# Moving a complex chunk scan from GpSimd to VectorE beside a ScalarE-paced attention

## The chip, the cores and the metric

The kernel runs on one NeuronCore of a Trainium2 chip. The metric is the device time of one execution in microseconds (us); smaller is better. Every run is repeated, and the kernel before runs beside it on the same chip. Engines are named as in the profile: PE is TensorE, PEld its weight loads, DVE VectorE, ACT ScalarE, POOL GpSimd, SPq the queue of DMA issues on SyncE.

## The reference

The output mixes two branches of the same input `x` (2048 positions, 512 channels, bf16):

```python
g = sigmoid((x * gate_w).sum(-1, keepdims=True))
a = softmax_attention(x, wqkv, heads=32, Dh=16) @ wo       # no mask, 2048 x 2048 scores per head
b = causal_conv(x, K) + x * Dskip                          # an S4 state-space convolution
#   K[d, l] = Re( sum_n C[d,n] * exp(dt[d] * A[d,n] * l) * dt[d] * B[d,n] ),  n = 0..127
return g * a + (1 - g) * b
```

Attention needs 32 x 2048 x 2048 exponentials. The convolution is done in 32 chunks of 64 positions. With `lam = exp(dt*A)`, a state of 128 complex numbers per channel is carried from chunk to chunk: `G <- mu * G + S[c]`, where `mu = lam^64` and `S[c]` is the contribution of chunk c. Inside a chunk the 64 taps of `K` are used directly.

## The kernel before

A small scheduler in the kernel writes the order of every engine. There are 512 steps. Each has a fixed attention part: two 128x1024 exponentials on ScalarE, the score matmuls of the next step, the value matmuls of the step before. What the convolution needs is squeezed in between by threads that ask for TensorE, VectorE or GpSimd time (`yield ("DVE", .7)`), for an event (`AFTER`), for a step (`Q`) or for the one free PSUM bank `MB` (`LOCK`). The engines then run their lists in order, each waiting on semaphores. Step numbers in this text are the scheduler's; times are the trace's.

```python
for q in range(NQ):                      # NQ = 512
    ex(2 * q)                            # ScalarE, 128x1024
    if q + 1 < NQ: qk(q + 1)             # TensorE: scores into PSUM banks SC
    ex(2 * q + 1)
    rate = dict(PE=.62 if q > 50 else 1.0, DVE=1.5, POOL=1.8)
    ...                                  # pv(q-1): values into PSUM bank OA; every 16 steps norm()
    sch.step(rate)                       # the convolution's threads
```

The threads that matter, in order of time:

```python
def base(qr, eng, k, c1):    # powers lam^0..15 of one quarter (128 channels), f32; quarter 0 on DVE, 1 to 3 on POOL
    ...
def table():                 # per block of 32 channels (16 blocks): lam^0..63 into PT, bf16, on DVE
    for blk in range(NBLK):
        ...
        for m in range(1, 4):
            for part in range(2):
                yield ("DVE", 1.05)      # three 128x512 bf16 tensor_tensor
                ...
def kstage(blk):             # taps K = Re(W * lam^l): 32 matmuls of 128 columns into MB, evicted to Kst, 8 DMAs
    ...
def sstage(blk):             # chunk sums S: 4 banks of MB per block, each evicted to Sst and sent to memory
    for bank in range(4):
        yield ("LOCK", "MB")
        yield ("PE", .6)
        ...                                          # 4 matmuls Ut x Qt into MB
        yield ("DVE", .7)
        op("DVE", ... v.tensor_copy(Sst(512 * (bank % 2), [[1, 512]]), MB(0, [[1, 512]])) ...)
        sch.unlock("MB")
        dma("SP", ... sd.dram(...), Sst(512 * (bank % 2), ...))
def weigh():                 # DVE: SW = W * S for four chunks at a time, 6 f32 operations
    ...
def scan():                  # POOL: per chunk s2 = G*Re(mu); s3 = swap(G)*Im(mu); s2 += SW; G = s2 + s3; SG = bf16(G)
    ...
def ystage():                # per block: 16 pairs k; for each 1 matmul Uy x Tt and 4 matmuls SG x Py into MB
    ...                      # two column groups of the array at a time
def ublocks():               # reversed copies of x, built by GpSimd
    for qr in range(4):
        ...                                          # 2 DMAs into X2
        yield ("Q", 2 + 8 * qr)
        for par in range(2):
            yield ("POOL", 3.0)
            op("POOL", ... g.tensor_copy(UB(...), X2(...)))
def gate():
    yield ("Q", 8)
    for lt in range(16):
        dma("SP", ... xg <- 128 rows of x)           # two buffers
        yield ("DVE", .7)
        op("DVE", ... gp[lt] = sum(xg * gw))
    op("ACT", ... ge = Exp(-gp))                     # one small exponential in ScalarE's list
    ...
    yield ("AFTER", "scan2", 0)
    for lt in range(16):
        dma("SP", ... xh <- 128 rows of x)           # two buffers
        yield ("POOL", 1.2)
        op("POOL", ... xD[lt] = xh * Dskip)
```

`SG`, the scanned states, has two buffers for four quarters: the states of quarter 2 may be loaded only when the output taps of quarter 0 (blocks y0 to y3) are done, those of quarter 3 after y4 to y7.

The softmax here doesn't subtract the row's maximum and nothing guards it: scores larger than these inputs give would overflow.

## Time and profile before

The kernel takes 1259.88 us (median of 3 runs, 1259.55 to 1261.51).

| | before |
|---|---|
| profiled span, mean TensorE clock | 1261.5 us, 0.565 |
| busy: TensorE, VectorE, ScalarE, GpSimd | 818.9, 664.4, 967.4, 622.4 us |
| ScalarE idle just before attention's exponentials | 263.9 us, of it 230.7 until scores came |
| one step where nothing disturbs | about 1.835 us, so 512 steps take about 940 us |
| before the first exponential, after the last | 17.8 us, 13.3 us |

No engine is busy all the time, yet one sets the pace. The page of the kernel before, first the busy times, then four of its costliest groups (line, engine, operation, count; busy us, mean ns of one; idle time of that engine just before them and what ended it):

```profile
span 1261.5 us, 16332 instructions
...
PE 818.9 (65%) x6378; PEld 247.3 (20%) x6400; DVE 664.4 (53%) x958; ACT 967.4 (77%) x1032; POOL 622.4 (49%) x704
...
L519 ACT ACTIVATE ET<-SC 128x1024 bf16<-128x1024 f32 x1024 | 960.9, 1067 | 263.9 <-PE SC L426 230.7
...
L842 POOL TENSOR_TENSOR s_143<-G,MI 128x256 f32<-128x256 f32 x120 | 104.1, 868 | 0.0
...
L812 DVE SCALAR_TENSOR_TENSOR SW<-SW,sw_145 128x512 f32<-128x512 f32 (+1 forms) x64 | 51.5, 843 | 0.0
```

The first group is the pace: 1024 exponentials, 961 us, and 264 us in which ScalarE stood before one of them. Nearly all those waits were for scores, that is for TensorE. The waits say why TensorE was late (who waited for whom: us in total, times, longest):

```profile
ACT ET L519 <- PE SC L426: 230.7, 81, 17.0
...
PEld MB L426 <- DVE Sst L757: 105.1, 62, 10.8
...
DVE Sst L757 <- DMA gm_sd<-Sst: 20.8, 7, 6.5
```

TensorE works in order, so a convolution matmul that waits for the bank `MB` to be emptied by VectorE also holds up the scores behind it. And VectorE was late partly because of GpSimd. The same bf16 128x512 product of the table, grouped by shape, in the kernel before: first on blocks whose tables were made while GpSimd scanned, then on blocks while it was idle:

```profile
L544 DVE TENSOR_TENSOR tt_134<-B_130,D_116 128x512 bf16<-128x512 bf16 x8 | 7.2, 902 | 0.0
...
L544 DVE TENSOR_TENSOR tt_134<-B_128,D_116 128x512 bf16<-128x512 bf16 x8 | 3.4, 419 | 0.0
```

The page "SBUF — State Buffer" of the Trainium skill, section "Who interferes with whom", says that a VectorE instruction with two SBUF inputs contends with a GpSimd instruction that reads SBUF, and that one with at most one SBUF input, outside VectorE's 2-port modes, does not. This trace agrees: the two-input product takes 902 ns instead of 419, while the evictions from PSUM (`Sst`) take 0.69 us with GpSimd busy or idle.

### The profile page before, as it was taken

To read this page: it belongs to the slowest core of one execution; us is meant where nothing else is said; L and a number is where in the kernel's file an instruction comes from. 1 tells how busy PE (TensorE), PEld (TensorE's weight loads), DVE (VectorE), ACT (ScalarE), POOL (GpSimd) and SP (SyncE) were. 2 spreads that over 40 slices of the span, in tenths; PEclk is the share of its full clock that TensorE was granted. 3 is DMA by queue.
4 is the path that set the end of the run, shared out by engine and by line. 5 is a ranking of instruction groups with operands and counts; after the bars stand their busy time and mean duration, and the time that the engine had idled before them with its cause. 6 is when DMAs were issued, how large, how long until landed. Compare 5 with 4: busy or idle time off the path is not lost.

```text
span 1261.5 us, 16332 instructions
## 1 busy us (share of the span) xinstructions
PE 818.9 (65%) x6378; PEld 247.3 (20%) x6400; DVE 664.4 (53%) x958; ACT 967.4 (77%) x1032; POOL 622.4 (49%) x704
## 2 busy tenths in 40 slices
PE   5554665666766545456457898576489559967665
PEld 1111111111111111011112343231034114311111
DVE  5999883664566778977862010544454511041101
ACT  5545666987988667677669988479679778999995
POOL 3799770000009888889830000899999984000000
PEclk9867656755555555555555555555555555557855
DMA  9551001266753443122343546336024205100000
GB/s 218 107 128 44 1 8 51 69 196 166 155 151 72 111 102 92 46 81 63 88 121 92 161 112 136 81 105 140 0 59 118 63 17 150 27 5 26 22 1 17
DMA packets 227550, 107.30 MB, mean 85 GB/s; under 512 B 190097, under 2 KB 217233, under 8 KB 223377
## 3 DMA queue, kind: packets, MB, share of 16 engines
q1 hardware_dynamic: 225744, 104.55, 33.1%
q10 hardware_dynamic: 1728, 1.70, 0.5%
q8 instruction: 50, 0.82, 0.3%
q14 instruction: 28, 0.22, 0.1%
HBM read 42.34 MB, written 35.85 MB: 62 GB/s over the span
## 4 chain that ended last, share of the span: by engine, by line
DVE 36%; POOL 18%; PE 18%; ACT 17%; DMA 5%; issue 3%; SPq 2%; ACTq 0%; DVEq 0%; POOLq 0%
ACT ET L519 17%; PE MB L426 8%; PE SC L426 5%; DVE SW L800 4%; PE OA L426 4%; DVE sw_145 L805 4%; POOL s_142 L839 4%; POOL G L848 4%; POOL s_142 L845 4%; DVE tt_133 L544 4%; DVE tt_134 L544 4%; DVE PT L544 3%; POOL s_143 L842 3%; DMA gm_sd<-Sst 2%; DVE pt_115 L544 2%
## 5 line engine op out<-in xcount | busy, mean ns | idle before, releaser
L519 ACT ACTIVATE ET<-SC 128x1024 bf16<-128x1024 f32 x1024 | 960.9, 1067 | 263.9 <-PE SC L426 230.7
L426 PE MATMUL SC<-Qm,KT 32*128 32x512 bf16 x2048 | 300.0, 576 | 181.1 <-ACT ET L519 165.8
L426 PE MATMUL OA<-ET,VE 128*32 128x512 bf16 x2048 | 296.6, 583 | 23.4 <-DVE OT L534 22.2
L426 PEld LDWEIGHTS SC<-Qm,KT 32*128 32x128 bf16 x2048 | 55.2, 98 | 372.3 <-ACT ET L519 323.6
L842 POOL TENSOR_TENSOR s_143<-G,MI 128x256 f32<-128x256 f32 x120 | 104.1, 868 | 0.0
L845 POOL TENSOR_TENSOR s_142<-s_142,SW 128x256 f32<-128x256 f32 x120 | 103.5, 862 | 0.0
L848 POOL TENSOR_TENSOR G<-s_142,s_143 128x256 f32<-128x256 f32 x120 | 97.2, 810 | 9.3
L839 POOL TENSOR_TENSOR s_142<-G,MU 128x256 f32<-128x256 f32 x120 | 101.5, 845 | 0.0
L426 PE MATMUL MB<-Qt,Ut 128*64 128x256 bf16 x256 | 40.8, 420 | 91.6 <-DVE Sst L757 72.2
L534 DVE STREAM_TRANSPOSE OT<-OA 128x512 f32<-128x512 f32 x32 | 22.8, 713 | 142.5 <-PE OA L426 142.5
L426 PEld LDWEIGHTS OA<-ET,VE 128*32 128x32 bf16 x2048 | 54.1, 101 | 221.1 <-issue 193.0
L426 PE MATMUL MB<-Tt,Uy 128*64 128x64 bf16 x256 | 66.9, 261 | 31.3 <-DVE Yst L905 30.6
L773 POOL MEMSET SG_139<- 128x256 bf16 x2 | 0.6, 311 | 174.9 <-PE MB L426 174.9
L757 DVE CAST Sst<-MB 128x512 bf16<-128x512 f32 x64 | 44.1, 689 | 63.9 <-PE MB L426 43.1
L905 DVE CAST Yst<-MB 128x512 bf16<-128x512 f32 x16 | 11.0, 689 | 111.2 <-PE MB L426 111.2
L800 DVE TENSOR_TENSOR SW<-SG_140,WR 128x512 f32<-128x512 bf16 (+1 forms) x32 | 33.2, 1076 | 65.2 <-POOL SG_140 L851 54.7
L836 POOL COPY G<-SW 128x256 f32<-128x256 f32 x4 | 4.8, 1200 | 121.0 <-DVE SW L812 120.7
L800 DVE TENSOR_TENSOR SW<-SG_139,WR 128x512 f32<-128x512 bf16 (+1 forms) x32 | 29.6, 965 | 64.3 <-POOL SG_139 L851 45.0
L544 DVE TENSOR_TENSOR PT<-tt_133,tt_134 128x512 bf16<-128x512 bf16 x96 | 53.2, 554 | 3.3
L426 PE MATMUL MB<-Py,SG_140 128*32 128x64 bf16 x512 | 46.4, 271 | 8.6 <-POOL SG_140 L851 8.6
L426 PE MATMUL MB<-xT,Wk 128*128 128x512 bf16 x59 | 23.9, 495 | 42.7 <-DVE KT L492 15.6
L812 DVE SCALAR_TENSOR_TENSOR SW<-SW,sw_145 128x512 f32<-128x512 f32 (+1 forms) x64 | 51.5, 843 | 0.0
(192 smaller groups left out, 985.7 us busy)
## 6 DMA issues: line engine op xcount, KB each, us to landing
gm_ptd<-PT SPq DMA_DIRECT2D x16, 1024.0 KB
Py<-gm_ptd SPq DMA_DIRECT2D x16, 1024.0 KB
gm_sd<-Sst SPq DMA_DIRECT2D x64, 128.0 KB
X_146<-gm_xrd SPq DMA_DIRECT2D x8, 512.0 KB
gm_ud<-UB SPq DMA_DIRECT2D x4, 1024.0 KB
Ut<-gm_ud SPq DMA_DIRECT2D x16, 256.0 KB
Uy<-gm_ud SPq DMA_DIRECT2D x16, 256.0 KB
Tt<-gm_kpd SPq DMA_DIRECT2D x32, 128.0 KB
```

What stands on the lines that cost most here:

```text
L426: op("PE", lambda t: t.matmul(out(), lhsT(), rhs(), start=start, stop=stop, skip_group_check=True, **kw), R, W)
L519: op("ACT", lambda a: a.activation(ET(1024 * e, [[1, 1024]]), sc(0, [[1, 1024]]), AF.Exp, scale=DH ** -0.5), [(sc, 0, h // 2), (sc, 1, h / ...
L534: op("DVE", lambda v: v.transpose(OT(o, [[1, 512]]), OA(0, [[1, 512]])), [(OA, 0, b)], [(OT, 0, b)])
L544: op(eng, lambda v: v.tensor_tensor(o(), a(), b_(), f), R, W)
L757: op("DVE", lambda v, bank=bank: v.tensor_copy(Sst(512 * (bank % 2), [[1, 512]]), MB(0, [[1, 512]])), [(MB, 0, ('S', blk, bank))], [(Sst, ...
L800: op("DVE", lambda v, so=so, o=o, nc_=nc_, ri=ri: v.tensor_tensor(SW(o + 128 * ri, [[256, nc_], [1, 128]]), sg(so + 128 * ri, [[256, nc_], ...
L805: op("DVE", lambda v, so=so, nc_=nc_, ri=ri: v.tensor_tensor(sw2(128 * ri, [[256, nc_], [1, 128]]), sg(so + 128 * (1 - ri), [[256, nc_], [ ...
L812: op("DVE", lambda v, d=d, x=x, ri=ri: v.scalar_tensor_tensor(d(), d(), -1.0 if ri else 1.0, x(), ALU.mult, ALU.subtract), [(SW, (sl, ri), ...
L839: op(e, lambda v: v.tensor_tensor(s2(0, [[128, 2], [1, 128]]), G(0, [[128, 2], [1, 128]]), MU(d0, [[0, 2], [1, 128]]), ALU.mult), key("G", ...
L842: op(e, lambda v: v.tensor_tensor(s3(0, [[128, 2], [1, 128]]), G(128, [[-128, 2], [1, 128]]), MI(d0, [[D, 2], [1, 128]]), ALU.mult), key(" ...
L845: op(e, lambda v, o=o: v.tensor_tensor(s2(0, [[1, 256]]), s2(0, [[1, 256]]), SW(o, [[1, 256]]), ALU.add), [(s2, 0)] + swk, [(s2, 0)])
L848: op(e, lambda v: v.tensor_tensor(G(0, [[1, 256]]), s2(0, [[1, 256]]), s3(0, [[1, 256]]), ALU.add), [(s2, 0), (s3, 0)], [(G, 0)])
```

## The change

The intent: take the scan and the powers away from GpSimd, so that VectorE is no longer slowed; pay for VectorE's extra work by deleting the weighing pass; and shorten TensorE's small matmuls. The weight is removed by folding its complex square root `V` into the power table: if every entry is `V * lam^j`, then a chunk sum times an output tap carries `V * V = W` by itself. That needs a complex square root (two ScalarE `Sqrt`, one VectorE reciprocal) and a sign change of the imaginary half, which is done while `Sst` is evicted. The diff cut to its core:

```diff
-def base(qr, eng, k, c1):
+def base(qr, eng, c1):
...
-        op(eng, lambda v: v.memset(FP(0, ...), 1.0), ...)          # lam^0, lam^1
-        op(eng, lambda v: v.tensor_copy(FP(1, ...), B["L1"](d0, ...)), ...)
+        for l, n in ((0, "VV"), (1, "VL")):                         # V, V*lam
+            op(eng, lambda v, l=l, n=n: v.tensor_copy(FP(l, ...), B[n](d0, ...)), ...)
...
     def params():
+        ...
+        op("ACT", lambda a: a.activation(B["u3"](0, [[1, D]]), B["u1"](0, [[1, D]]), AF.Sqrt), ...)
+        ...
+        yield ("Q", p.q + 2)
+        yield ("DVE", .7)
+        tt("DVE", full("u1"), full("u2"), full("u3"), ALU.add, ...)
+        op("ACT", lambda a: a.activation(B["u3"](0, [[1, D]]), B["u1"](0, [[1, D]]), AF.Sqrt, scale=.5), ...)
+        ...
+        op("DVE", lambda v: v.reciprocal(B["u1"](0, [[1, D]]), B["u3"](0, [[1, D]])), ...)
...
     def table():
-                    yield ("DVE", 1.05)
+                    yield ("DVE", 1.27)
...
     def kstage(blk):             # 8 matmuls of 512 columns instead of 32 of 128, 1 DMA instead of 8
-        for k0 in range(0, 16, 4):
+        for part, wn in ((0, "wrb"), (1, "nwi")):
+            for a in range(4):
+                mm(lambda a=a: MB(0, [[1, 512]], 32 * a, 32), ...)
...
     def sstage(blk):
-            op("DVE", ... v.tensor_copy(Sst(512 * (bank % 2), [[1, 512]]), MB(0, [[1, 512]])) ...)
+            op("DVE", ... v.tensor_copy(Sst(..., [[256, 2], [1, 128]]), MB(0, [[256, 2], [1, 128]])) ...)
+            op("DVE", ... v.tensor_scalar(Sst(... + 128, [[256, 2], [1, 128]]), MB(128, ...), -1.0, None, ALU.mult) ...)
...
-    def weigh():                                                    # deleted, 40 lines
     def scan():
-                e = "POOL"
+        e = "DVE"
+            for bl in range(4):
+                yield ("AFTER", f"sg{4 * qr + bl}", 4)
...
     def ystage():                # half blocks; per q: 2 matmuls Uy x Tt, then 8 of SG x Py over four column groups
-                for par in range(2):
-                    for ri in range(2):
+                for ri in range(2):
+                    for j in range(4):
...
     def gate():
-        yield ("AFTER", "scan2", 0)
+        yield ("AFTER", "S15", 0)
...
-    for th in (projs(), params(), base(0, "DVE", 0, .00105), table(), weigh(), scan(), ystage(), ...):
+    for th in (projs(), params(), scan(), bases(), table(), ystage(), ublocks(), gate(), combine(), outs()):
...
-        rate = dict(PE=.62 if q > 50 else 1.0, DVE=1.5, POOL=1.8)
+        rate = dict(PE=.62 if q > 50 else 1.0, DVE=1.65, POOL=1.8)
```

The tables now wait for the powers of all four quarters (`base3`), not only of their own.

## The prediction

> **What bounds the kernel now.** ScalarE paces it: 512 steps of two 128x1024 exponentials. Where nothing disturbs them (timeline, last 80 us) a pair takes 1.84 us, so 512 take about 940 us, plus 18 us of head and 13 us of tail: a floor near 970 us. The page's groups show 264 us of ScalarE idle before these exponentials, 231 of them ended by TensorE's scores. TensorE (819 us busy, clock 0.565) runs in order and stalls at the bank MB until VectorE empties it (waits: 105 us for Sst, 31 Yst, 35 KT). VectorE is late mostly because of GpSimd. From windows and timeline, per 16 steps (floor 29.4 us): steps 0-63, powers on both engines, 44 to 56 us; steps 64-143, tables and chunk sums, 29 to 37; steps 144-239, GpSimd scan with VectorE weighing, 39 to 49; taps (y) 33 to 36; one reload of SG at 768-791 us, 50.
>
> **GpSimd's cost to VectorE.** A bf16 128x512 tensor_tensor takes 0.42 us alone, 0.84 overlapped by GpSimd; f32 128x1024 1.22 against 2.6; the weighing products 0.68 against 1.2. The Trainium skill ("SBUF — State Buffer", Who interferes with whom) says that a VectorE instruction with two SBUF inputs contends with a GpSimd instruction that reads SBUF; this trace agrees.
>
> **Removed.** 409 us of GpSimd scan, about 110 us of GpSimd powers, VectorE's 132 us of weighing, the doubling by overlap, and on TensorE 384 narrow matmuls (40 us busy become about 18).
> **Added.** The scan on VectorE: estimated from its 128x256/512 operations 0.33 to 0.43 us each, about 1.75 us per chunk, 124 chunks, 215 us. Three more quarters of powers, about 25 us each; a square root of the weight, about 15 us; two ScalarE square roots, with up to four table loads of 1.28 us. Sst's eviction becomes two operations, 0.69 to 0.85 us.
>
> **What lies on the path.** By the program's order and uncontended durations, VectorE needs 22 to 31 us per 16 steps nearly everywhere (38 in the first 16): about ScalarE's 29.4. So:
> - steps 0-15: about 48; 16-95: 31 to 36 (before 29 to 56);
> - tables and chunk sums: 31 to 32; scans 32 to 33, since VectorE about equals ScalarE;
> - taps: 10 small matmuls cost 0.97 us in pairs now; four column groups at once should need about 0.5, so a step (0.54+0.54+0.5) drops under 1.84: 31 to 32;
> - given back: scans 2 and 3 each start 4 steps after the taps that free their SG buffer, while the reload needs about 20 us; each loses some 8 to 12 us (before only once); scans 0 and 1 a few us;
> - tail: five output tiles in one bank now stand after the last exponential: about +13 us.
> Sum: about 1105 us, 12% less.
>
> Predicted 1105 us, 8 in 10 between 1055 and 1165. Faster by over 2%: 0.94; within 2%: 0.04; slower: 0.02.
>
> **What would show it.** GpSimd busy under 110 us; bf16 table products at 0.42 us throughout; ScalarE idle near 130 us; scan windows at 31-34 us per 16 steps, taps at 30-33; two idle ScalarE stretches at starts of scans 2 and 3; 24-28 us after the last exponential.
>
> **What would make it wrong.** VectorE's scan slower than 1.75 us per chunk, stalling each softmax normalization; the SP queue filled by twice as many tap loads (about 13 of 15 us per block); chunk-sum stages staying at 2.2 us per step through the Sst handoff.

## The result, and the profile after

The changed kernel takes 1168.95 us (median of 4 runs, 1164.44 to 1170.63), and its result is correct. The ratio to the kernel before is 0.927 (95% interval 0.924 to 0.930). Ratios here are the mean time of one kernel's fast runs over that of the other's of the same rounds, so not quite the ratio of the medians quoted. The gain is 91 us, where the prediction had 155. The direction was right; the time lies just outside the range of 1055 to 1165.

The page after, the same groups:

```profile
span 1168.8 us, 15477 instructions
...
PE 755.2 (65%) x5997; PEld 204.7 (18%) x6016; DVE 671.8 (57%) x1525; ACT 978.9 (84%) x1039; POOL 64.4 (6%) x36
...
L515 ACT ACTIVATE ET<-SC 128x1024 bf16<-128x1024 f32 x1024 | 965.5, 1104 | 120.0 <-PE SC L422 107.9
...
L829 DVE TENSOR_TENSOR G<-s_138,s_139 128x256 f32<-128x256 f32 x120 | 51.0, 425 | 4.1
```

VectorE does the whole scan and is hardly busier than before (672 us against 664), because the weighing and the doubled durations are gone. ScalarE's idle time before attention's exponentials fell from 264 to 120 us. The mean clock granted to TensorE was 0.591, against 0.565 before; no run tells what that is worth, but the scan windows below show no higher clock after (0.50) than before (0.53). The waits:

```profile
ACT ET L515 <- PE SC L422: 107.9, 49, 8.5
PEld MB L422 <- DVE Sst L780: 81.4, 61, 5.6
...
DVE Sst L778 <- DMA gm_sd<-Sst: 30.5, 12, 4.3
...
DVE G L819 <- DMA SG_136<-gm_sd: 19.5, 2, 17.8
...
ACT ge L945 <- DVE gp L941: 17.6, 1, 17.6
DVE G L819 <- DMA SG_135<-gm_sd: 17.2, 1, 17.2
```

Two of these stand out: a VectorE wait of 17 to 18 us for reloaded states at each of two scans, which was predicted (before there was one such wait, of 19.3 us), and a single ScalarE wait of 17.6 us for the gate (5.5 us before), which was not. The table product of the kernel after, by shape, no longer depends on the block:

```profile
L540 DVE TENSOR_TENSOR tt_131<-B_128,D_119 128x512 bf16<-128x512 bf16 x8 | 3.4, 419 | 0.0
```

Where the time went is best seen by steps. The starts of the exponentials cut the trace into stretches; the predicted column is worked out from the prediction's figures per 16 steps (the middle of a range where it gave one; for "taps, scans 2 and 3" nine windows of 31.5 and three of 32.5, plus 20 for the two reloads). The columns of the trace add up to the spans within 0.2 us; the predicted one adds up to about 1100, not quite the 1105 of the prediction's own sum.

| steps (stage in the kernel after) | before, us | predicted | after, us | after minus predicted |
|---|---|---|---|---|
| head | 17.8 | 18 | 17.9 | 0 |
| 0-15 | 52.0 | 48 | 68.5 | +20 |
| 16-95 (powers, first tables) | 212.5 | 167 | 159.0 | -8 |
| 96-111 (gate) | 37.4 | 31.5 | 47.9 | +16 |
| 112-143, 176-207, 240-287 (chunk sums) | 247.8 | 220 | 257.8 | +38 |
| 144-175, 208-239 (scans 0 and 1) | 176.9 | 130 | 117.3 | -13 |
| 288-479 (taps, scans 2 and 3) | 444.8 | 401 | 417.9 | +17 |
| 480-511 | 59.0 | 59 | 60.4 | +1 |
| after the last exponential | 13.3 | 26 | 22.3 | -4 |

The gain of 93 us between the two profiles is the sum of about 140 us won in steps 16-95, in the scans and in the taps, and about 47 us lost in the other rows. (The rows are steps, and in the kernel before other work stood at some of them.) The windows of the trace show the scan, before and then after, for the same steps 224 to 239 (the stretch in us, then the busy time of each engine in it). In the kernel before:

```profile
596.80:645.90 49.10, 22.10 (x204) 5.53 (x204) 37.75 (x52) 29.68 (x32) 41.16 (x55) 0.53 0.31 92
```

In the kernel after, this scan, then a stretch of chunk sums, then one of output taps:

```profile
core 0: us, PE busy (x) PEld busy (x) DVE busy (x) ACT busy (x) POOL busy (x), PEclk, DMA share, GB/s
529.10:558.40 29.30, 18.42 (x132) 3.39 (x131) 28.17 (x81) 29.30 (x33) 0.00 (x0) 0.50 0.00 1
558.40:595.90 37.50, 22.67 (x182) 5.15 (x180) 24.52 (x66) 29.93 (x33) 0.00 (x0) 0.59 0.49 142
850.70:882.70 32.00, 27.92 (x292) 10.91 (x288) 3.42 (x8) 32.00 (x34) 0.00 (x0) 0.50 0.47 115
```

In the scan, VectorE is busy for 28.2 of 29.3 us and ScalarE never stands still: the stage is at its floor. In the chunk sums, 37.5 us are spent on 29.9 us of exponentials, though VectorE is busy for only 24.5. The question is where the losses come from.

**The first losses.** The timeline of the kernel after from 35.5 us (start, duration, engine, what; idle time before it and what ended it):

```profile
35.50 1.28 ACT L600 ACT_TABLE_LOAD   x1
...
36.74 7.64 POOL L926 COPY UB<-X_140 64x2048 bf16<-64x2048 bf16 x2 [23.95 <-DMA X_140<-gm_xrd]
36.84 4.07 DVE L540 TENSOR_TENSOR u_99<-zr 128x512 f32<-128x512 f32 x1
...
40.84 4.10 DVE L540 TENSOR_TENSOR u_100<-zi 128x512 f32<-128x512 f32 x1
...
45.46 0.68 DVE L598 SCALAR_TENSOR_TENSOR u_99<-u_99,u_100 128x512 f32<-128x512 f32 x1
46.17 0.63 ACT L600 ACTIVATE u_101<-u_99 128x512 f32<-128x512 f32 x1 [9.39 <-DVE u_99 L598]
...
46.80 1.28 ACT L515 ACT_TABLE_LOAD   x1
48.10 3.77 ACT L515 ACTIVATE ET<-SC 128x1024 bf16<-128x1024 f32 x4
```

The two squares take 4.07 and 4.10 us beside GpSimd's two copies; the other products of this shape around them take 0.68. ScalarE has the square root next in its list and stands 9.4 us for it, with exponentials behind it. The second root costs 9.6 us at step 9. There a copy does only a part of it: the first three gate sums stand before the root's operand in VectorE's list, they wait 2.5 us for a load, and one of them takes 3.87 us beside a copy instead of 0.69. In e5 below, where the gate is moved away and the copies stay, this second wait is 3.5 us.

**The gate.** ScalarE's list in the kernel after, around step 105:

```profile
256.36 7.54 ACT L515 ACTIVATE ET<-SC 128x1024 bf16<-128x1024 f32 x8
281.46 0.21 ACT L945 ACTIVATE ge<-gp 128x16 f32<-128x16 f32 x1 [17.55 <-DVE gp L941]
```

A 0.2 us exponential waits 17.6 us for VectorE, which in turn waits 19.2 us in all for the `xg` loads (9 waits) of its sixteen gate sums. Twelve of the sixteen stand in one clump from 259.7 to 281.4 us. In the kernel before there was a clump too, from 184 to 208 us, but ScalarE waited only 5.5 us for it.

**The chunk sums.** One bank and the next of the kernel after:

```profile
451.97 0.42 DVE L778 CAST Sst<-MB 128x256 bf16<-128x256 f32 x1 [2.38 <-DMA gm_sd<-Sst]
452.31 0.41 DVE L780 TENSOR_SCALAR Sst<-MB 128x256 bf16<-128x256 f32 x1
...
452.78 0.64 PE L422 MATMUL MB<-Qt,Ut 128*64 128x256 bf16 x4 [2.40 <-DVE Sst L780]
...
454.00 8.36 ACT L515 ACTIVATE ET<-SC 128x1024 bf16<-128x1024 f32 x9 [2.76 <-PE SC L422]
```

VectorE waited 2.4 us for the DMA that still read the `Sst` buffer, TensorE waited 2.4 us for VectorE, and ScalarE 2.8 us for the scores behind.

### The profile page after: what moved, and what is told of

It reads as the page before. It is cut to its first block, busy times and chain, and to the rows that moved or that the text cites. A ratio compares the mean times of both kernels' runs of the same rounds, so it can differ in the third digit from the quotient of the medians.

```text
span 1168.8 us, 15477 instructions
## 1 busy us (share of the span) xinstructions
PE 755.2 (65%) x5997; PEld 204.7 (18%) x6016; DVE 671.8 (57%) x1525; ACT 978.9 (84%) x1039; POOL 64.4 (6%) x36
## 4 chain that ended last, share of the span: by engine, by line
DVE 35%; ACT 34%; PE 10%; DMA 10%; SPq 6%; issue 2%; POOL 1%; another core or an unknown queue 0%; ACTq 0%; DVEq 0%; POOLq 0%
ACT ET L515 34%; DVE G L829 4%; PE MB L422 4%; DMA gm_sd<-Sst 4%; PE SC L422 4%; DVE s_138 L827 4%; DVE s_138 L822 3%; DVE s_139 L824 3%; PE OA L422 2%; DVE tt_130 L540 2%; DVE PT L540 2%; DMA xg<-in_A_x_dram 2%; DVE tt_131 L540 2%; DVE SG_136 L831 2%; DVE SG_135 L831 2%
## 5 line engine op out<-in xcount | busy, mean ns | idle before, releaser
L422 PEld LDWEIGHTS SC<-Qm,KT 32*128 32x128 bf16 x2048 | 54.9, 97 | 453.5 <-ACT ET L515 417.9
L890 DVE CAST Yst<-MB 128x256 bf16<-128x256 f32 x32 | 13.4, 420 | 177.0 <-PE MB L422 177.0
L778 DVE CAST Sst<-MB 128x256 bf16<-128x256 f32 x64 | 27.0, 421 | 60.8 <-DMA gm_sd<-Sst 30.5
L829 DVE TENSOR_TENSOR G<-s_138,s_139 128x256 f32<-128x256 f32 x120 | 51.0, 425 | 4.1
L422 PE MATMUL MB<-Tt,Uy 128*64 128x64 bf16 x256 | 33.7, 260 | 29.8 <-DVE Yst L890 15.6
L822 DVE TENSOR_TENSOR s_138<-G,MU 128x256 f32<-128x256 f32 x120 | 50.1, 417 | 0.1
L824 DVE TENSOR_TENSOR s_139<-G,MU 128x256 f32<-128x256 f32 x120 | 50.1, 418 | 0.0
L540 DVE TENSOR_TENSOR PT<-tt_130,tt_131 128x512 bf16<-128x512 bf16 x96 | 40.8, 425 | 3.3
L956 POOL TENSOR_TENSOR xD<-xh,Dsk 128x512 bf16<-128x512 bf16 x16 | 19.6, 1244 | 397.4 <-DMA xh<-in_A_x_dram 397.4
L926 POOL COPY UB<-X_140 64x2048 bf16<-64x2048 bf16 x8 | 31.4, 3920 | 49.7 <-DMA X_140<-gm_xrd 49.2
L422 PEld LDWEIGHTS MB<-Tt,Uy 128*64 128x64 bf16 x256 | 16.9, 127 | 83.5 <-issue 67.8
L422 PE MATMUL MB<-Py,SG_136 128*32 128x64 bf16 x512 | 29.9, 314 | 0.0
L422 PE MATMUL MB<-Py,SG_135 128*32 128x64 bf16 x512 | 29.9, 314 | 0.0
```

The lines of the kernel that those rows point to most:

```text
L422: op("PE", lambda t: t.matmul(out(), lhsT(), rhs(), start=start, stop=stop, skip_group_check=True, **kw), R, W)
L540: op(eng, lambda v: v.tensor_tensor(o(), a(), b_(), f), R, W)
L778: op("DVE", lambda v, bank=bank: v.tensor_copy(Sst(512 * (bank % 2), [[256, 2], [1, 128]]), MB(0, [[256, 2], [1, 128]])), [(MB, 0, ('S', b ...
L822: op(e, lambda v: v.tensor_tensor(s2(0, [[128, 2], [1, 128]]), G(0, [[128, 2], [1, 128]]), MU(d0, [[0, 2], [1, 128]]), ALU.mult), key("G", ...
L824: op(e, lambda v: v.tensor_tensor(s3(0, [[128, 2], [1, 128]]), G(128, [[-128, 2], [1, 128]]), MU(D + d0, [[D, 2], [1, 128]]), ALU.mult), k ...
L829: op(e, lambda v: v.tensor_tensor(G(0, [[1, 256]]), s2(0, [[1, 256]]), s3(0, [[1, 256]]), ALU.add), [(s2, 0), (s3, 0)], [(G, 0)])
```

## The experiments

Twelve kernels ran; all gave correct results. Times are medians of 4 runs; "excess" is the time of a stretch minus 1.835 us per step. After has an excess of 192 us in all. Each edit is against the kernel after unless it says otherwise. The theories: for the first 20 steps, A, that GpSimd's remaining copies block VectorE, against B, that the square roots are placed too early in ScalarE's list; for step 105, C1, that only the place of the gate's small exponential stalls ScalarE, against C2, that VectorE is held up by the gate's loads and would stall ScalarE in any case; for the chunk sums, D1, that the two `Sst` buffers are too few, against D2, that VectorE's own work, above all the table, stands in front of the evictions.

### e2_copies_dve: the eight copies on VectorE

```diff
-                yield ("POOL", 3.0)
-                op("POOL", lambda g, par=par: g.tensor_copy(UB(...
+                yield ("DVE", 1.3)
+                op("DVE", lambda g, par=par: g.tensor_copy(UB(...
```

> The eight UB copies are moved from GpSimd to VectorE; nothing else changes. Theory A (GpSimd copies block VectorE's two-input operations in the first 20 steps, each 4 us long, and everything behind them in order): steps 0-19, 84 us in the changed kernel against a floor of 37, fall by 20 to 30 us, so the time falls to about 1140-1150 us. Rival B (it is ScalarE, which waits in its own order for the operands of its two square roots and reloads tables, whoever makes VectorE late): they fall by under 8 us, time 1160-1169.

Measured: 1171.82 us, ratio 0.929 (0.928 to 0.931). Steps 0-19 fell from 84.4 to 60.2 us, the waits for the two roots from 9.4 and 9.6 to 2.6 and 5.4 us: theory A's cause is real and worth 24 us in its stage. The total did not move, where A had expected 1140 to 1150. ScalarE's waits in this run:

```profile
ACT ge L945 <- DVE gp L941: 34.1, 1, 34.1
```

The gate's stall grew from 17.6 to 34.1 us. By the table's rows the chunk sums lost another 9.6 us and the tail 5.7, and the taps gave 4.4 back. The gain was handed to later stages.

### e3_sqrt_late: both square roots four steps later

```diff
+        yield ("Q", p.q + 4)
         op("ACT", ... AF.Sqrt), key("u1"), key("u3"))
...
+        yield ("Q", p.q + 4)
         op("ACT", ... AF.Sqrt, scale=.5), key("u1"), key("u3"))
```

> The two square roots are put into ScalarE's order 4 steps later than now, so that VectorE has long finished their operands; the GpSimd copies stay. Theory A (the GpSimd copies hold VectorE, and TensorE then waits for bank MB anyway): the two waits of 9.5 us before the square roots vanish from ScalarE's own list but reappear in part as waits for TensorE's scores; steps 0-19 fall by 5 to 12 us. Rival B (the order on ScalarE is the cause): they fall by 18 to 20 us, time about 1150 us.

Measured: 1173.43 us, ratio 0.930 (0.929 to 0.932). The waits for the roots vanished, but steps 0-19 took 85.3 us, as before: ScalarE now waited for scores (7.7 and 8.7 us), and the gate, whose VectorE work moved forward into the freed budget, stalled 15.8 us at step 15. In the kernel after, that stall stands at step 105 and not in these steps. Less that stall they took 69.5 us, 15 less than 84.4: more than the 5 to 12 that A allowed, less than the 18 to 20 of B. So this run does not decide between the two alone. That waits for scores came where the roots had waited speaks for A, and e2 shows the copies' share without touching the roots. The total rose because the chunk sums became slower, as in e5 below.

### e4_ge_late: the gate's exponential twelve steps later

```diff
         sch.mark("gp")
+        yield ("Q", p.q + 12)
         op("ACT", ... ge = Exp(-gp) ...)
```

> The gate's exponential is put into ScalarE's order 12 steps later. Theory C1 (ScalarE's order makes the stall of 17.6 us at step 105): the stall vanishes, time falls by about 17 us to 1152. Rival C2 (VectorE waits in its order for the gate's loads, the loads stand in the SP queue behind transposes, and TensorE waits 18.9 us for VectorE's eviction of MB): ScalarE's wait changes its name to TensorE's scores, time falls by under 5 us, 1164-1169.

Measured: 1166.6 us, ratio 0.926 (0.924 to 0.928). The timeline of ScalarE in this kernel:

```profile
257.97 7.55 ACT L515 ACTIVATE ET<-SC 128x1024 bf16<-128x1024 f32 x8
283.10 3.77 ACT L515 ACTIVATE ET<-SC 128x1024 bf16<-128x1024 f32 x4 [17.59 <-PE SC L422]
```

The same 17.6 us, now ended by scores. C1 falls, C2 stands: VectorE, waiting for the gate's loads, keeps `MB` occupied (the one wait of TensorE for `Kst`, 18.9 us in the kernel after, is there, with 17.9 us), and scores queue behind.

### e5_gate_paced: the gate spread over sixteen steps, one load each

```diff
-        yield ("Q", 8)
+        yield ("Q", 50)
         for lt in range(16):
+            yield ("Q", p.q + 1)
...
         sch.mark("gp")
+        yield ("Q", p.q + 4)
...
-    for th in (projs(), params(), scan(), bases(), table(), ystage(), ublocks(), gate(), ...):
+    for th in (projs(), params(), gate(), scan(), bases(), table(), ystage(), ublocks(), ...):
```

> The gate's 16 products are done from step 50 on, one per step at most, before the tables begin, with the exponential 4 steps later: loads come when the SP queue is empty. If the stall at step 105 is made by those loads (C2), it vanishes without another in its place: steps 96-105 fall from 36 us to 19, time about 1150-1154 us. If the stall has another cause, time stays at 1165-1170.

Measured: 1160.41 us, ratio 0.921 (0.919 to 0.922). The stall at step 105 is gone, and steps 0-19 took 75.4 us. But the three stretches of chunk sums got slower, their excess rising from 54 us to about 75, so more than half of what was won was lost again. Why they got slower was not taken apart. The pacing of the gate itself need not be the reason: in e3, where the gate is not paced but the chunk sums also begin about three steps earlier, their excess is as high, about 78 us.

### e1_sst3: three Sst buffers instead of two

```diff
-    sb("Sst", 2 * 512)
+    sb("Sst", 3 * 512)
...
-            op("DVE", ... v.tensor_copy(Sst(512 * (bank % 2), ...
+            op("DVE", ... v.tensor_copy(Sst(512 * ((4 * blk + bank) % 3), ...
```

> Three staging buffers Sst in place of two (no room for four). Theory D1 (a bank's staging is written again only when its store has landed, 3.8 us, while a bank comes every 1.83 us step; VectorE waits 30.5 us in all for it, and TensorE and ScalarE behind it): these waits of VectorE fall below 8 us and the chunk-sum stages lose 20 to 30 us of their 54 us over ScalarE's pace; time 1140-1150. Rival D2 (the handover of the single bank MB between TensorE and a late VectorE makes the loss; the store only comes last): the waits move to TensorE's wait for Sst, and the time falls by under 8 us, 1161-1169.

Measured: 1156.87 us, ratio 0.918 (0.916 to 0.919), 12 us better than the kernel after. The waits for `Sst` in this run:

```profile
PEld MB L422 <- DVE Sst L780: 65.5, 61, 5.7
...
PE MB L422 <- DVE Sst L780: 37.3, 31, 5.2
DVE Sst L778 <- DMA gm_sd<-Sst: 6.8, 5, 2.1
```

VectorE's wait for the DMA fell from 30.5 to 6.8 us and the chunk sums' excess from 54 to about 39. The buffers are a part, between what D1 and D2 expected; TensorE still waits for the eviction.

### e10_table_spread: e1, and the table planned more thinly

Against e1_sst3, so that fewer table products stand in front of an eviction:

```diff
-                    yield ("DVE", 1.27)
+                    yield ("DVE", 1.55)
```

> On top of three staging buffers, the plan counts a table product triple as 1.55 instead of 1.27 us, so that the same VectorE work is spread over about 17 more steps. Theory D2 for what the third buffer left (VectorE is behind its plan when a bank of chunk sums must be emptied, and TensorE waits in order): the loss over ScalarE's pace in the three chunk-sum stretches, about 39 us without the gate's stall, falls to under 22 us. The work ends 18 steps later, so the tail grows; total 1140-1165 us. Rival D3 (the bank's round trip costs the same even when VectorE is early): the loss stays at 33-42 us and the total rises to 1157-1172.

Measured: 1159.94 us, ratio 0.921 (0.920 to 0.923). The same waits in this run:

```profile
PEld MB L422 <- DVE Sst L780: 46.3, 52, 3.9
PE MB L422 <- DVE Sst L780: 22.9, 21, 3.4
```

The chunk sums' excess fell again, from about 39 to 26 us (a gate stall of 17.0 us that now falls into this stretch not counted): less than D2 expected (under 22), but clear of the 33 to 42 of its rival D3. VectorE's table work is thus a second part. The whole is not faster, since everything after moves later: the tail grew from 23.4 to 43.9 us. What makes up the remaining 26 us stays open.

### e6_xh_paced: the xh loads one every four steps

```diff
-            yield ("POOL", 1.2)
+            yield ("Q", p.q + 4)
             op("POOL", ... xD[lt] = xh * Dskip ...)
```

> The 16 loads of xh, each followed by a GpSimd product, are planned at least 4 steps apart instead of as fast as GpSimd's budget allows. Theory: in the first taps the SP queue stands at an xh load until GpSimd frees its buffer, so the tap loads come late (three ScalarE stalls of 3.4 to 5.5 us between 703 and 735 us). Then these three vanish and the time falls by 11 to 15 us, to 1154-1158. Rival: twice as many tap loads fill the SP queue by themselves; then two of the three stay and the time falls by under 5 us.

Measured: 1163.49 us, ratio 0.923 (0.921 to 0.924). The three stalls in the first taps (5.5, 3.4 and 5.4 us at steps 306, 311 and 314) vanished, and the excess of y0 to y3 fell from 18.6 to 6.2 us. The stall at scan 2 grew from 8.2 to 15.8 us, with the later loads now issued there. Half was handed on.

### e7_scan23_after_y7: the third scan planned after output block 7

```diff
+            if qr == 2:
+                yield ("AFTER", "y7", 0)
             for c in range(NCH - 1):
```

> The third scan waits in the plan until the taps of the second quarter are planned too, so that both SG buffers are reloaded while other work goes on. If the reloads make the two stalls (waits of 17 us on VectorE for SG, 8 us each on ScalarE), both vanish: time falls by 14 to 20 us, to about 1150-1155. If VectorE's rate in the scan makes them, ScalarE idles as long somewhere in these scans and the time stays within 1164-1170.

Measured: 1152.73 us, ratio 0.913 (0.911 to 0.915), 16 us better, as expected. VectorE's wait for reloaded states fell from 36.7 us (two kinds, in the kernel after) to:

```profile
DVE G L821 <- DMA SG<-gm_sd: 1.6, 1, 1.6
```

Scans 2 and 3 then ran at ScalarE's pace (excess 0.2 and 1.0 us). Of the stalls mended one at a time, this is the only one whose gain came back in full.

### e8_narrow_taps: the old order of the output taps

The half-blocks stay, and the eight small matmuls of each group of ten go in pairs of column groups again instead of over four:

```diff
-                for ri in range(2):
-                    for j in range(4):
+                    for par in range(2):
+                        j = 2 * p2 + par
...
+                        for ri in range(2):
```

> The y matmuls go back to the order of before (one tap product, then its four state products in two column groups); the rest is the changed kernel. A group of ten goes back from about 0.7 to 0.97 us, a step of taps from 1.97 to 2.06-2.2 us, 128 such steps: time rises by 12 to 25 us, to about 1181-1194. If the order is worth nothing, it stays within 1164-1173.

Measured: 1181.67 us, ratio 0.937 (0.936 to 0.939), so 12.7 us slower than the kernel after. A step with taps took 2.07 to 2.20 us instead of 1.97 to 2.03. The new order pays, but it was expected to bring such a step down to 1.84. This run also shows what the new order costs. Its exponentials in a stretch of taps (850 to 890 us):

```profile
L515 ACT ACTIVATE ET<-SC 128x1024 bf16<-128x1024 f32 x39 | 37.9, 1022 | 3.7 <-PE SC L422 1.5
```

With the old order they take 1022 ns and ScalarE waits between them; in the kernel after they take 1208 ns on average in the taps (shown in the next section) and ScalarE does not wait. (A part of this is that an exponential right behind another is recorded about 0.1 us longer than one after a wait, 1127 ns in the scans, so the next section compares their starts.)

### e9_scan_pool: the scan alone back on GpSimd

```diff
-        e = "DVE"
+        e = "POOL"
...
-                yield (e, .7)
+                yield (e, 1.3)
...
-                yield (e, .9)
+                yield (e, 1.65)
```

> The chunk scan alone goes back to GpSimd (without weighing, powers on VectorE): tells what moving the scan was worth. A chunk then takes 3.4 to 3.9 us in a chain, a quarter about 115 us, in parallel with other work; VectorE's two-input operations double where they overlap. If freeing VectorE of GpSimd's reads is the gain: time 1200-1250. If the missing weighing pass is the gain and the scan's engine matters little, 1160-1180.

Measured: 1208.42 us, ratio 0.958 (0.957 to 0.960). Two groups of this run:

```profile
L540 DVE TENSOR_TENSOR tt<-B,D 128x512 bf16<-128x512 bf16 x192 | 112.2, 624 | 2.4
L822 POOL TENSOR_TENSOR s<-G,MU 128x256 f32<-128x256 f32 x120 | 95.1, 793 | 0.3
```

The table products are back at 624 ns on average, against 0.42 us on every block in the kernel after, and a scan operation takes 793 ns instead of 417. TensorE's waits for `Sst` grew with it (from 53.7 to 102.4 us before matmuls), while it waited only 16.8 us for the scanned states, so it is VectorE's slowness more than the scan's own length that costs. Beside the rest of the change, moving the scan is worth 39.5 us of the 91, as a balance: by the table's rows chunk sums and scans 0 and 1 lost 81 us, and taps and tail gave 41 back. If the parts simply add, the other 52 us belong to the rest: no weighing, the powers on VectorE, and the taps, of whose new order e8 measured 13.

### c1_all and c2_all: the remedies together

c1_all joins e1, e2, e3, e5, e6 and e7, and lets the last output tiles in sooner (TensorE rate 0.9 after step 482).

> All together: three staging buffers, copies on VectorE, late square roots, paced gate, paced xh, third scan after the second quarter's taps, and output tiles planned faster at the end. If each stall is a cause of its own, the gains add up (24 + 17 + 12 + 13 + 16 + 9 us) to about 1075-1095 us. If they only hand on the same loss (as the copies' gain went into the gate's stall), it stays above 1110.

Measured: 1104.92 us, ratio 0.876 (0.874 to 0.878), 64 us better than the kernel after, and between the two outcomes expected. The six single edits add up to 35 us (12.1 - 2.9 - 4.5 + 8.5 + 5.5 + 16.2). The late output rate was never tried alone, so not all of the surplus need be joint effect. A stall of 12.4 us at step 117 was left, where the late copies waited for their loads, and the tail was 29.0 us.

c2_all adds to it: the copies' thread right after the gate, at least eight steps after each load; the scan planned a little thinner; the output tiles after the last exponential rotated over five banks.

```diff
-            yield ("Q", 2 + 8 * qr)
+            yield ("Q", max(p.q + 8, 24 + 10 * qr))
...
-                yield (e, .7)
+                yield (e, .75)
...
-                yield (e, .9)
+                yield (e, .95)
...
+            if p.q >= NQ:
+                yield from outproj(lt, [(SC[0], 0, 0), (SC[1], 0, 0), (SC[2], 0, 0), (OA, 0, 0), (MB, 0, 0)][lt % 5])
+                continue
```

> The combination once more, with what its trace left: the copies for the tap blocks planned before the powers and paced (a 12 us stall at step 117), scan operations counted 6% dearer in the plan (about 5 us at the end of each of the first two scans), and output tiles after the last exponential rotated over five banks instead of one (2.8 us a tile becomes about 1.9). If these are the causes, 1070-1092 us; if the stalls only move again, 1095-1115.

Measured: 1090.44 us, ratio 0.866 (0.865 to 0.868), the fastest version, 78.5 us below the kernel after. Its three additions were not tried apart. Its group of exponentials, to be read against 120.0 us of idle time after and 263.9 before:

```profile
L515 ACT ACTIVATE ET<-SC 128x1024 bf16<-128x1024 f32 x1024 | 967.2, 1106 | 69.3 <-PE SC L422 63.5
```

## Why the prediction was right or wrong

**Right.** The engine that bounds (ScalarE, floor near 970 us) and the mechanism: GpSimd slowed VectorE, VectorE held `MB`, TensorE stalled, ScalarE starved. GpSimd's busy time fell to 64 us (under 110 predicted), the table products are at 0.42 us throughout, a scan chunk takes 1.79 us on VectorE (1.75), and 22.3 us follow the last exponential (just under the 24 to 28 given). e9 shows that moving the scan pays by itself. Idle time of 120 us before the exponentials is near the 130 given, although the total missed; that count leaves out the waits of the roots and of the gate, which stand before other ScalarE instructions, and the longer exponentials of the taps. Both reload stalls came: 8.2 us at scan 2 and 7.3 at scan 3, the scans' excess being 9.7 and 10.2 (8 to 12 each predicted), and e7 confirmed their cause.

**Better than predicted, by 13 us.** Scans 0 and 1: "32 to 33" per 16 steps were 29.3. VectorE is busy for 28.2 us of these and still keeps up.

**Wrong: steps 0-15, 20 us.** The prediction gave "about 48"; it was 68.5. It counted VectorE's work at uncontended durations ("38 in the first 16"), and counted "the doubling by overlap" as removed. But the change removes only the scan and the powers; the copies of `ublocks()` stay, 31 us of GpSimd, and in the first steps they meet exactly the new VectorE work that ScalarE's new square roots wait for. The trace shows 4.07 us for a 0.68 us product, and e2 took 24 us off steps 0-19 by moving the copies. The gate's first sums, in front of the second root, add to it: e5, which moved the gate away, took 9 us off the same steps.

**Wrong: the gate, 16 us.** The term "16-95: 31 to 36" was right on average (31.8 per 16 steps, from 39.6 falling to 29.3), but what comes next had no term for the gate at all. The gate exists in both kernels, and the trace of before showed a wait of 5.5 us for it; with the changed order most of its loads and sums stand at step 105, and 17.6 us of ScalarE's time went there. e4 shows that the clump, not the place of the small exponential, is the cause; e5 removed the stall by spreading it.

**Wrong: the chunk sums, 38 us, the largest term.** "Tables and chunk sums: 31 to 32" were 36.0 to 37.6. The reasoning was that VectorE's busy time, 22 to 31 us per 16 steps, fits within ScalarE's 29.4. It does: VectorE is busy for 24.5 us of the 37.5 in the window shown. What counts is when it gets to the eviction. The missing term is the handover of `MB`: e1 measured the two `Sst` buffers at 15 us of excess (12 us of time), e10 the table products in front of the eviction at another 12 or 13; 26 remain unexplained. The prediction had named this ("chunk-sum stages staying at 2.2 us per step through the Sst handoff") among what would make it wrong, and they stayed at 2.25 to 2.35. So the step that failed is "VectorE needs 22 to 31 us per 16 steps ... about ScalarE's 29.4", taken for the time of the stage.

**Wrong: the taps, 17 us with scans 2 and 3.** Two waits had no term. The moved `xh` loads, 12 us by e6: the prediction named the SP queue as a danger, but only for twice as many tap loads, not for these. And where scans 2 and 3 end, at steps 363 and 423, ScalarE stands 5.2 and 5.4 us: TensorE waits 4.9 and 5.1 us until VectorE empties `MB` of taps (`Yst`), an eviction that stands behind the last scan operations in VectorE's list. It is the handover again. The scans' pace of 29.3 instead of 32 to 33, and reloads that cost less than 20, took a part back.

The taps themselves came out near their "31 to 32" per 16 steps (31.5 to 33.1 in windows without a stall), but not for the reason given, so that hit is partly luck: steps under 1.84 would have been 29.4, and what the rest was for is not said. A step with taps took 1.97 to 2.03 us instead. The ten small matmuls were to need "about 0.5" us and show 0.66 in the timeline. Yet in the taps' window above TensorE is busy for 27.9 of 32.0 us, while ScalarE is busy for all 32.0: its own exponentials got longer, for which the prediction had no term. In the kernel after, first in that taps window, then in the scan window:

```profile
L515 ACT ACTIVATE ET<-SC 128x1024 bf16<-128x1024 f32 x34 | 34.4, 1208 | 0.0
```

```profile
L515 ACT ACTIVATE ET<-SC 128x1024 bf16<-128x1024 f32 x33 | 30.5, 1127 | 0.0
```

The new order of the taps lengthens them, as the traces show. From the first exponential of a step, beside which the small matmuls run, to the second, the median over some 110 steps with taps is 1.08 us in the kernel after and 0.92 in e8, whose edit is the order alone. It is 0.92 in the kernel before, too, which has the old order, and 1.07 to 1.09 in all the other runs, which have the new one. Over the taps this adds up to 16.6 us, and 0.16 us is the middle of what a step with taps takes above 1.84. So the failed step is "(0.54+0.54+0.5)": it summed TensorE's time alone and took ScalarE's for fixed. What in the four column groups at once slows an exponential beside them was not tested.

The common fault, the longer exponentials aside, is one of method: the sum compared an engine's work per 16 steps with the pace. That fits where an engine flows (the scans), and fails where an engine must answer in time (an eviction, a root, a gate sum in an in-order list).

## What to carry to other kernels

When work leaves an engine that disturbs another, list what stays on it and check which new instructions will run beside that. Beside a pacing engine that runs in order, comparing busy time is enough only for work that no one waits for; each handover needs its own check of buffers, of the loads before it in the same queue, and of what stands in front of it. Expect a single mended stall to be handed on to the next (24 us at the stage gave nothing in the total in e2), look whether an order that is faster on one engine lengthens what runs beside it (here 0.92 to 1.08 us), and judge remedies together: here six of them, with a sooner output, gave 64 us, where their single gains sum to 35.

## What the Trainium skill lacked or had wrong

- "SBUF — State Buffer", section "Who interferes with whom", was right and of use: beyond the doubled table products (902 against 419 ns), its statement that the loser of the shared port pair fully blocks fits the 4.07 us that a 0.68 us VectorE product took beside a GpSimd copy of about 3.9 us. Its last consequence, "PE and ACT never wait on anyone", is about SBUF ports; neither it nor any page I found has a word on what made 128x1024 exponentials from PSUM take 1208 ns in the tap windows and 1127 in the scan windows, with ScalarE never idle in either. The runs show that small matmuls over four column groups do it: beside them the next exponential started after 1.08 us, beside the same matmuls in pairs after 0.92 (e8).
- "ScalarE: Activation LUTs", "What ACT_TABLE_LOAD costs", gives about 1283 ns for the load plus about 1380 ns of drain for every switch. Here the load took 1.28 us, but no drain is seen in the trace: the root ends at 46.80 us, the load runs for 1.28 us, and the next exponential starts at 48.10.
- "GPSIMD Engine Reference", section 3.1, states a ratio of 1.96 between GpSimd and VectorE for a tensor_tensor. The scan's operations agree: 793 to 868 ns on GpSimd, 417 to 425 on VectorE.
- I found no page that tells how long a VectorE reciprocal takes; the f32 128x512 one here took 3.34 us, about five times the 0.68 us of a product of that shape.
